# A spectral mixer on one core: the filter on four k1 low at once with 32x32 tiles, and the last two transforms in the other order

## The chip, the core and the metric

The kernel runs on one NeuronCore of a Trainium2 chip. The metric is the time of one execution on the device in microseconds, the median of several runs. The core's engines run side by side, each with its own queue of instructions: PE (TensorE, matmuls), DVE (VectorE), ACT (ScalarE), POOL (GpSimd) and SP (which here only issues transfers). PE reads from SBUF and writes to PSUM, which has eight banks of 128 partitions x 512 float32.

## The reference

The input x has 2048 tokens of 512 channels. Both branches start from its layer norm, and their product is added to x:

```
xn = layernorm(x)
s  = irfft2(rfft2(xn) * (w_r + 1j * w_i))          # over tokens and channels
h  = layernorm(xn)
u  = gelu(einsum("sd,sf->df", h, w1) + b1)          # mixing over the tokens, F = 1792
g  = silu((u @ w2 + b2).T)
out = x + s * g
```

## The kernel before

Tokens are split as 128 partitions times 16 tiles j (2048 = 128 x 16), so that the transform over the sequence falls into two steps: one of 128 points over the partitions, with the frequency k1 = 16 hi + lo (hi 0 to 3, lo 0 to 15, real and imaginary rows), and one of 16 points over j. The channel transform is done on 128 folded rows in four groups. The products with w1 and w2 are made from operands split in a high and a low part (float32r), three products for each; those of the spectral branch are plain float32, apart from the last transform.

First stage (16 passes, one for each j). Layer norm, the first seven of the 14 tiles of u (`hidden_early`, L335), the 128-point transform of h (`first_transform`, L207), and `fold`, whose two writes on DVE (L228) and two on POOL (L223, L224) leave the rows in `ey`.

Middle stage. PE works at two things in turn. `hidden_rest` gives the other seven tiles of u, as 32 parts of w1 (`w1_part`) with three or four groups of three products each (`mm3`, L118 to L120), prepared three parts ahead: a copy on ACT for the high half and a subtraction on DVE for the low one (`split`, L115). `filter_steps` is the filter of one of the 16 k1 low, in four steps: the channel transform (four matmuls of 128 columns, L446) and its copy by ACT (L448); the 16-point transform over j, one 128x128 matmul of 512 columns (L454), whose matrix `gf` serves all four hi at once; two half-height copies by ACT that swap real and imaginary rows (L456, L457); twelve operations on DVE that weight the rows (L465 to L482), with two more copies by ACT (L483, L484); and the transform back over j (four matmuls of 128 columns, L505), which ACT copies to `ey` (L506). A list of steps with weights says after which filter step how many groups of `hidden_rest` come, in the order of the code; the scheduler then orders the instructions of each engine.

Last stage (eight passes p over output tiles p and p + 8). Seven products of 21 matmuls with forms of w2 (L768); `w2_form` makes them from loads of w2 on SP (L609) and adding loads on POOL (L611). Between them stand, for each of 16 tiles j, `gathered` (a copy of the rows of tile j by ACT, L693), `channels` (the inverse channel transform, four matmuls, L700, and nine operations on DVE with a split, L115), `spectral` (the inverse 128-point transform as three float32r products, L118 to L120 again), and `finish`, which multiplies with the gate from PSUM (L739) and adds the tile to the output by a transfer on POOL (L741).

Of the kernel before, what the change touches and what calls it, by code (L numbers as in the profile page):

```python
# [8 lines left out]
F32 = mybir.dt.float32  # L9
# [15 lines left out]
TAIL = 2  # L25
# [4 lines left out]
RT = float(np.sqrt(0.5))  # L30

def _round12(a):
    m, e = np.frexp(a)
    return np.ldexp(np.round(m * 4096.0) / 4096.0, e)


def _parts(a, axis):
    hi = _round12(a)  # L40
    return np.stack([hi, a - hi], axis).astype(np.float32)


def _constants():
    q = np.arange(P)
    f = np.zeros((P, P))
    for lo in range(16):
        for hi in range(4):
            k = 16 * hi + lo
            a = 2 * np.pi * ((q * k) % P) / P  # L50
            f[:, lo * 8 + hi] = np.cos(a)
            f[:, lo * 8 + 4 + hi] = np.cos(np.pi * q) if k == 0 else np.sin(a)
# [19 lines left out]
    g = np.zeros((16, P, P))  # L72
    freq = np.zeros((P, 16), int)
    j = np.arange(16)
    for lo in range(16):
        for hi in range(4):
            k1 = 16 * hi + lo
            for r in range(16):
                re, im = r * 4 + hi, 64 + r * 4 + hi
                cr, sr = j * 8 + hi, j * 8 + 4 + hi  # L80
                if k1:
                    k = k1 + 128 * r
                    th = 2 * np.pi * ((j * k) % S) / S
                    g[lo, cr, re], g[lo, sr, re] = np.cos(th), -np.sin(th)
                    g[lo, cr, im], g[lo, sr, im] = -np.sin(th), -np.cos(th)
                    freq[[re, im], lo] = k
                elif r == 0:
                    g[lo, cr, re], g[lo, cr, im] = 1.0, np.cos(np.pi * j)
                    freq[im, lo] = S // 2
                else:  # L90
                    k = 128 * r if r < 8 else 64 + 128 * (r - 8)
                    rows = cr if r < 8 else sr
                    th = 2 * np.pi * ((j * k) % S) / S
                    g[lo, rows, re], g[lo, rows, im] = np.cos(th), -np.sin(th)
                    freq[[re, im], lo] = k
    c = {
        "c_f": f.astype(np.float32),
        "c_ft": _parts(f.T, 1),
        "c_d": fd.reshape(4, P, P).transpose(1, 0, 2).astype(np.float32),
        "c_i": iv.transpose(1, 0, 2).astype(np.float32),  # L100
        "c_g": g.astype(np.float32),
        "c_h": g.transpose(0, 2, 1).astype(np.float32),
# [4 lines left out]
def spectral_mixer_kernel(tc, x, w1, b1, w2, b2, wk, we, wx, c_f, c_ft, c_d, c_i, c_g, c_h, out):  # L107
# [14 lines left out]
    with tc.tile_pool(name="ps", bufs=1, space=PSUM) as psp, ExitStack() as left, ExitStack() as right:  # L122
# [463 lines left out]
        for step, lag in steps:  # L586
# [4 lines left out]
            if slot % 2:  # L591
                form_step()
# [250 lines left out]
```

## Time and profile before

| what | value |
|---|---|
| time, median of 3 runs | 394.23 us (394.01 to 394.5) |
| profiled execution, its span | 390.9 us |
| first stage | 0 to about 96 us |
| middle stage, filter and most hidden products | about 96 to 208 us |
| end of the hidden products, first forms | about 208 to 219 us |
| last stage, eight passes | about 219 us to the end, 20.7 us a pass |

The profiled execution's own time is its span; the median of the runs lies 3.3 us above it. A line such as L454 is line 454 of the kernel before. In a group's row stand the engine, the operation, the tiles written and read, the shape and the count, then busy time and the mean duration of one in ns, then the idle time of the engine ahead of it and what ended it. A stretch's row gives busy time and count for PE, PE's weight loads, DVE, ACT and POOL, then the granted clock, the share of the DMA engines and GB/s. A row of the chain gives start, length and what ran.

### The profile page before, as it was taken

What the parts mean: (1) busy time and instruction counts of PE and PEld (TensorE: products, weight loads), DVE (VectorE), ACT (ScalarE), POOL (GpSimd) and SP (SyncE); (2) the same over time, 40 slices, a digit from 0 to 9 for tenths busy, and PEclk for the clock granted to TensorE, in tenths of its full rate; (3) what the DMA queues carried; (4) which work ended last, traced back from release to release, by engine and by line L of the source; (5) the groups of instructions that cost most, each with busy time, mean ns of one, the idle gap of its engine ahead of it and who ended that gap; (6) DMA issues with size and microseconds to landing.
All of it is one profiled execution on the core that took longest, in us unless ns stands there. A gap on an engine that the chain in (4) does not pass through costs nothing.

```text
span 390.9 us, 7102 instructions
## 1 busy us (share of the span) xinstructions
PE 383.5 (98%) x2456; PEld 338.9 (87%) x2456; DVE 327.9 (84%) x776; ACT 248.3 (64%) x455; POOL 59.0 (15%) x109
## 2 busy tenths in 40 slices
PE   8999999999999999999999999999999999999995
PEld 4888888888787887788878889999999999999994
DVE  6899998866699989978898879797879788787974
ACT  4677665575987665687667486565646474656542
POOL 2133332322100000000011003020202011110200
PEclk9999999999999999999999999999999999999999
DMA  8957457213545535653637459887868778685602
GB/s 267 311 171 249 146 199 247 71 34 101 181 139 170 181 111 172 177 180 114 190 109 230 94 192 230 175 215 155 229 131 234 147 217 162 197 152 168 110 9 54
DMA packets 35016, 64.72 MB, mean 166 GB/s; under 512 B 4194, under 2 KB 19426, under 8 KB 34852
## 3 DMA queue, kind: packets, MB, share of 16 engines
q1 hardware_dynamic: 30292, 52.40, 42.1%
q0 software_dynamic: 4688, 11.86, 18.0%
q8 instruction: 19, 0.31, 0.3%
q14 instruction: 17, 0.14, 0.1%
HBM read 60.05 MB, written 8.13 MB: 174 GB/s over the span
## 4 chain that ended last, share of the span: by engine, by line
PE 88%; ACT 4%; DVE 4%; DMA 1%; issue 1%; SPq 0%; POOL 0%; DVEq 0%; ACTq 0%; POOLq 0%
PE ps L768 32%; PE ps L335 20%; PE ps L119 6%; PE ps L118 6%; PE ps L120 6%; PE ps L207 4%; PE ps L700 3%; PE ps L446 3%; PE ps L454 3%; PE ps L505 3%; PE ps L324 1%; ACT w2f L620 1%; DMA a<-in_w_dram 1%; DVE w2f L621 1%; ACT u L267 1%
## 5 line engine op out<-in xcount | busy, mean ns | idle before, releaser
L335 PE MATMUL ps<-h,w1h 128*128 128x512 f32 x224 | 58.5, 398 | 0.0
L118 PE MATMUL ps<-h,w1h 128*128 128x512 f32 x112 | 50.4, 451 | 0.1
L621 DVE TENSOR_TENSOR w2f<-s,w2f 128x896 fp32r<-128x896 f32 x32 | 34.8, 1092 | 17.5 <-ACT w2f L620 16.8
L335 PEld LDWEIGHTS ps<-h,w1h 128*128 128x128 f32 x224 | 40.9, 188 | 7.9
L120 PE MATMUL ps<-h,w1l 128*128 128x512 f32 x112 | 45.3, 405 | 0.0
L119 PE MATMUL ps<-h,w1h 128*128 128x512 f32 x112 | 44.3, 396 | 0.0
L768 PE MATMUL ps<-fa,w2f 128*128 128x256 f32 x336 | 43.4, 282 | 0.1
L768 PE MATMUL ps<-fb,w2f 128*128 128x256 f32 x336 | 42.7, 281 | 0.1
L768 PEld LDWEIGHTS ps<-fa,w2f 128*128 128x128 f32 x336 | 41.4, 188 | 0.9 <-DVE w2f L621 0.3
L768 PEld LDWEIGHTS ps<-fb,w2f 128*128 128x128 f32 x336 | 40.5, 188 | 0.5 <-DVE c L735 0.5
L768 PE MATMUL ps<-fc,w2f 128*128 128x256 f32 x336 | 40.7, 279 | 0.0
L768 PEld LDWEIGHTS ps<-fc,w2f 128*128 128x128 f32 x336 | 40.0, 188 | 0.0
L620 ACT ACTIVATE w2f<-s 128x896 fp32r<-128x896 f32 x32 | 30.2, 947 | 14.0 <-DVE s L634 10.3
L621 DVE TENSOR_TENSOR w2f<-a,w2f 128x896 fp32r<-128x896 f32 x24 | 26.0, 1085 | 6.1 <-ACT w2f L620 6.0
L620 ACT ACTIVATE w2f<-a 128x896 fp32r<-128x896 f32 x24 | 22.8, 950 | 12.7 <-PE ps L768 8.7
L335 PE MATMUL ps<-h,w1l 128*128 128x512 f32 x112 | 30.6, 390 | 0.0
L611 POOL DMA_DIRECT2D s<-in_w_dram x16 | 13.9, 869 | 106.8 <-DVE es L705 45.7
L118 PEld LDWEIGHTS ps<-h,w1h 128*128 128x128 f32 x112 | 21.2, 189 | 6.2 <-issue 2.6
L119 PEld LDWEIGHTS ps<-h,w1h 128*128 128x128 f32 x112 | 21.2, 189 | 5.5 <-issue 2.6
L120 PEld LDWEIGHTS ps<-h,w1l 128*128 128x128 f32 x112 | 21.0, 188 | 5.4 <-issue 1.0
L335 PEld LDWEIGHTS ps<-h,w1l 128*128 128x128 f32 x112 | 21.0, 188 | 4.5
L330 DVE TENSOR_TENSOR w1l<-w1r,w1h 128x512 fp32r<-128x512 f32 (+1 forms) x32 | 20.6, 644 | 2.7 <-ACT w1h L327 2.6
(126 smaller groups left out, 784.2 us busy)
## 6 DMA issues: line engine op xcount, KB each, us to landing
a<-in_w_dram SPq DMA_DIRECT2D x24, 448.0 KB, 3.5
wt<-in_wk_dram SPq DMA_DIRECT2D x16, 512.0 KB, 3.7
s<-in_w_dram POOLq DMA_DIRECT2D x17, 448.0 KB, 6.4
s<-in_w_dram SPq DMA_DIRECT2D x15, 448.0 KB, 3.9
w1s<-in_w_dram SPq DMA_DIRECT2D x48, 128.0 KB, 2.5
w1r<-in_w_dram SPq DMA_DIRECT2D x16, 256.0 KB, 3.4
x<-in_x_dram SPq DMA_DIRECT2D x15, 256.0 KB, 3.6
out_dram<-in_x_dram SPq DMA_DIRECT2D x4, 960.0 KB, 6.7
```

The source lines that it names most:

```text
L118: T.matmul(o, lh, rh, start=first, stop=False)
L119: T.matmul(o, lh, rl, start=False, stop=False)
L120: T.matmul(o, ll, rh, start=False, stop=last)
L207: T.matmul(z[:, b], h[:, b * P:(b + 1) * P], c, start=True, stop=True)
L330: keep(V.tensor_sub(dst, src, hi.bitcast(F32)))
L335: T.matmul(ps[:, bank + i], w[wi][:, i * P:(i + 1) * P], hj, start=first and j == 0, stop=last and j == NJ - 1)
L446: T.matmul(pd[:, b * P:(b + 1) * P], eyl[:, b], cd[:, b], start=True, stop=True)
L454: T.matmul(px, gf, sh, start=True, stop=True)
L611: G.dma_start(t, w2_half(*added), accum_op=ALU.add)
L620: ordered(A.activation(wf[:, 0], v, AF.Copy))
L621: ordered(V.tensor_sub(wf[:, 1], v, wf[:, 0].bitcast(F32)))
L768: in_turn(j0, T.matmul(o, wf[:, wi, i], ui, start=m + a == 0 and n in (1, 2, 5), stop=m == NH - 1 and a == 2, skip_group_check=n in (6, 3, ...
```

## The change

The filter now takes the 16 k1 low in four groups of four (`QUADS`, `filter_quad`). The rows of `ey` are laid out so that the 16 j (real, imaginary) of one hi stand on 32 partitions. The transform over j is then, for each of four lo and four hi, a matmul of 32x32 with 512 columns; the one back is 32 such matmuls with 256 columns. Where real and imaginary rows had been swapped by half-height copies, ACT copies two PSUM banks at once (`e`) and two transfers on SP exchange even and odd rows into `z`. DVE weights half a group at a time. Of the 32 parts of w1, 16 keep the subtraction on DVE; the others get their low half as a negated copy by ACT, to which a transfer on POOL adds w1. In the last stage the rows of a tile are collected by eight transfers (`gathered`), the 128-point transform comes first and in plain float32 (`sequence`), the channel transform follows, and `finish` reads SBUF.

```diff
+QUADS = ((4, 5, 6, 7), (0, 1, 2, 3), (8, 9, 10, 11), (12, 13, 14, 15))
...
-        ey = pers.tile([P, 16, 4, 16, 8], F32, name="ey")
+        ey = pers.tile([P, 16, 4, 8, NJ], F32, name="ey")
+        eys = ey.rearrange("p l g h j -> p l (g h j)")
...
-                keep(V.scalar_tensor_tensor(ey[:, :, g, j, :], t[:, 0].rearrange("p (l c) -> p l c", c=8), sc,
-                                            o[:, 0].rearrange("p (l c) -> p l c", c=8), op0=ALU.mult, op1=ALU.add))
+                keep(V.scalar_tensor_tensor(ey[:, :, g, :, j], t[:, 0].rearrange("p (l h) -> p l h", h=8), sc,
+                                            o[:, 0].rearrange("p (l h) -> p l h", h=8),
+                                            op0=ALU.mult, op1=ALU.add))
...
-        def filter_steps(n, lo):
...
+        def filter_quad(n, los):
+            gf = mp.tile([P, 4, 32], F32, name=f"gf{n}", tag="gf")
+            SY.dma_start(gf, c_g[n].rearrange("p (q c) -> p q c", c=32))
+            for q, lo in enumerate(los):
+                pd = ps[:, 6 - q]
+                for b in range(4):
+                    T.matmul(pd[:, b * P:(b + 1) * P], ey[:, lo, b].rearrange("p h j -> p (h j)"), cd[:, b],
+                             start=True, stop=True)
+                A.activation(eys[:, lo].rearrange("p (s g c) -> p g s c", s=2, c=64),
+                             pd.rearrange("p (g s c) -> p g s c", s=2, c=64), AF.Copy)
+                yield
+            for q, lo in enumerate(los):
+                for hi in range(4):
+                    T.matmul(ps[32 * q:32 * q + 32, 3 + hi], gf[32 * hi:32 * hi + 32, q], eys[32 * hi:32 * hi + 32, lo],
+                             start=True, stop=True)
...
+            def swapped(h):
+                e, z = (mp.tile([P, 2, 2, 256], F32, name=f"{c}{n}_{h}", tag="ez", bufs=4) for c in "ez")
+                A.activation(e, ps[:, 3 + 2 * h:5 + 2 * h].rearrange("p b (s c) -> p b s c", s=2), AF.Copy)
+                SY.dma_start(z[0::2], e[1::2])
+                SY.dma_start(z[1::2], e[0::2])
+                return e, z
+            def weighted(h, e, z):
...
+                for i, w in enumerate((wa, wb)):
+                    SY.dma_start(w, wk[:, at:at + 2, i::2])
...
+                G.tensor_mul(s1[:, 0], z[:, :, :, 0], e1[:, at:at + 2])
+                G.tensor_mul(s1[:, 1], e[:, :, :, 0], e2[:, at:at + 2])
+                G.tensor_add(s1[:, 0], s1[:, 0], s1[:, 1])
+                V.scalar_tensor_tensor(pr, zi, sg[:, 0:1], er, op0=ALU.mult, op1=ALU.add)
+                V.scalar_tensor_tensor(pi, zr, sg[:, 0:1], ei, op0=ALU.mult, op1=ALU.subtract)
+                V.tensor_mul(pq, pq, wa)
+                V.tensor_add(pr, pr, pi)
+                V.scalar_tensor_tensor(er, zi, sg[:, 1:2], er, op0=ALU.mult, op1=ALU.add)
+                V.scalar_tensor_tensor(ei, zr, sg[:, 1:2], ei, op0=ALU.mult, op1=ALU.subtract)
+                V.tensor_mul(e, e, wb)
+                V.tensor_add(er, er, ei)
+                V.tensor_sub(pi, pr, er)
+                V.tensor_add(pr, pr, er)
+                V.tensor_copy(pq[:, :, :, 0], s1[:, 0])
...
+            weighted(0, *swapped(0))
             yield
+            half = swapped(1)
             yield
+            weighted(1, *half)
             yield
+            for s in range(2):
+                for hi in range(4):
+                    for q in range(4):
+                        rows = slice(32 * q, 32 * q + 32)
+                        T.matmul(ps[32 * hi:32 * hi + 32, 3 + q, 256 * s:256 * s + 256], hf[rows, hi, s],
+                                 back[hi // 2][rows, hi % 2, s], start=True, stop=True)
...
-                    w.append(w1_part(*parts_[i + 3][:2], True))
+                    w.append(w1_part(*parts_[i + 3][:2], i % 3 == 0 or i + 3 >= len(parts_) - LATE // 3))
...
+        slots = [(0, 2)] * 4 + [(0, 2), (0, 2)]
+        for n in range(1, 4):
+            slots += [(n, 3), (n - 1, 2)] + [(n, 4)] * 3 + [(n, 3), (n, 3), (n - 1, 1)]
+        slots += [(3, 16), (3, 0)]
...
         def gathered(j):
+            yj = fp.tile([P, D], F32, name=f"yj{j}", tag="yj", bufs=3)
+            for r in range(8):
+                SY.dma_start(yj[16 * r:16 * r + 16], eys[16 * r + j:16 * r + j + 1])
+            return yj
+
+        def sequence(j, yj):
+            pf = ps[:, j // NP].rearrange("p (b c) -> p b c", c=P)
+            for b in range(4):
+                in_turn(j, T.matmul(pf[:, b], yj[:, b * P:(b + 1) * P], cft, start=True, stop=True))
             yt = fp.tile([P, 4, P], F32, name=f"yt{j}", tag="yt", bufs=2)
-            A.activation(yt.rearrange("p b (l c) -> p b l c", c=8), ey[:, :, :, j, :].rearrange("p l b c -> p b l c"), AF.Copy)
+            A.activation(yt, pf, AF.Copy)
             return yt
...
-            split(ch, cl, y)
-            return ch, cl
-
-        def spectral(j, y):
-            mm3(ps[:, j // NP], cft[:, 0], cft[:, 1], *y, True, True)
+            return y
...
-            V.tensor_mul(g[:, cols], ps[:, j // NP, cols], g[:, cols])
+            V.tensor_mul(g[:, cols], y[:, cols], g[:, cols])
```

How the order moves on PE in the second half of the middle stage: the rows before, where `h` and `w1h`, `w1l` belong to the hidden products, `sh` and `gf` to the transform over j, `pq` and `hf` to the one back.

```order
L454 MATMUL ps<-sh_2327,gf_2250 128x512
L120 MATMUL ps<-h_94,w1l_7_2333 128x512
L118 MATMUL ps<-h_94,w1h_7_2332 128x512
L119 MATMUL ps<-h_94,w1h_7_2332 128x512
L120 MATMUL ps<-h_94,w1l_7_2333 128x512
L118 MATMUL ps<-h_95,w1h_8_2379 128x512
L119 MATMUL ps<-h_95,w1h_8_2379 128x512
L120 MATMUL ps<-h_95,w1l_8_2380 128x512
L505 MATMUL ps<-hf_2269,pq_2282 128x128 x4
L118 MATMUL ps<-h_95,w1h_8_2379 128x512
```

The same engine with the change (line numbers are those of the changed kernel: L121 to L123 are the hidden products, L461 the 32x32 matmuls forward, L517 those back), first where the third group of four goes forward, then where the second comes back.

```order
L123 MATMUL ps<-h_100,w1l_13_1807 128x512
L461 MATMUL ps<-ey,gf_1732 32x512 x16
L121 MATMUL ps<-h_100,w1h_13_1806 128x512
L122 MATMUL ps<-h_100,w1h_13_1806 128x512
L123 MATMUL ps<-h_100,w1l_13_1807 128x512
```

```order
L123 MATMUL ps<-h_101,w1l_14_1832 128x512
L517 MATMUL ps<-pq_0_1646,hf_1628 32x256 x8
L517 MATMUL ps<-pq_1_1760,hf_1628 32x256 x8
L517 MATMUL ps<-pq_0_1646,hf_1628 32x256 x8
L517 MATMUL ps<-pq_1_1760,hf_1628 32x256 x8
L121 MATMUL ps<-h_101,w1h_14_1831 128x512
```

Where single matmuls of one k1 low stood every few products, there are now 16 or 32 small ones in a row, four times each way.

PE with the change at the end of the middle stage, where the back transform of the last four stands (`pq_0` and `pq_1` are its halves) and the last hidden products follow:

```order
L121 MATMUL ps<-h_99,w1h_12_2345 128x512
L517 MATMUL ps<-pq_1_2273,hf_2152 32x256 x8
L517 MATMUL ps<-pq_0_2163,hf_2152 32x256 x8
L517 MATMUL ps<-pq_1_2273,hf_2152 32x256 x8
L123 MATMUL ps<-h_101,w1l_14_2450 128x512
L121 MATMUL ps<-h_102,w1h_15_2456 128x512
L122 MATMUL ps<-h_102,w1h_15_2456 128x512
```

Before, the last back transform has this place; 45 products follow it to the first product of the last stage, and 19 with the change:

```order
L505 MATMUL ps<-hf_2397,pq_2410 128x128 x4
L118 MATMUL ps<-h_98,w1h_11_2467 128x512
L119 MATMUL ps<-h_98,w1h_11_2467 128x512
L120 MATMUL ps<-h_98,w1l_11_2468 128x512
L118 MATMUL ps<-h_98,w1h_11_2467 128x512
```

The queue of SP in a pass of the last stage, before (`s` and `a` are loads of w2) and with the change (`yj` are the collected rows):

```order
L609 DMA a_2_2970<-in_w_dram 128x896
L609 DMA a_2_3002<-in_w_dram 128x896
L609 DMA s_11_3223<-in_w_dram 128x896
L609 DMA s_2_3030<-in_w_dram 128x896
L609 DMA a_10_3080<-in_w_dram 128x896
```

```order
L621 DMA a_2_2891<-in_w_dram 128x896
L621 DMA a_2_2921<-in_w_dram 128x896
L706 DMA yj_2923<-ey 16x1x512 x8
L621 DMA s_2_2958<-in_w_dram 128x896
L621 DMA a_10_3004<-in_w_dram 128x896
L706 DMA yj_3035<-ey 16x1x512 x8
L621 DMA s_11_3156<-in_w_dram 128x896
```

Sixteen transfers of 32 KB join five loads, and stand behind loads that wait for a free buffer.

More of the change, by code (lines that the diff above doesn't have):

```diff
@@ L24 @@
 WARM = 16
-TAIL = 2
 LATE = 12
@@ L82, in _constants @@
                     k = k1 + 128 * r
+                    if k1 == 0 and r > 7:
+                        k = 64 + 128 * (r - 8)
                     th = 2 * np.pi * ((j * k) % S) / S
[L84 to L95, printed above, removed]
+                    if k1:
+                        g[0, :, re], g[1, :, re] = np.cos(th), -np.sin(th)
+                        g[0, :, im], g[1, :, im] = -np.sin(th), -np.cos(th)
+                        at[[re, im]] = k
+                    elif r == 0:
+                        g[0, :, re], g[0, :, im] = 1.0, np.cos(np.pi * j)
+                        at[im] = S // 2
+                    else:
+                        one = 0 if r < 8 else 1
+                        g[one, :, re], g[one, :, im] = np.cos(th), -np.sin(th)
+                        at[[re, im]] = k
@@ L96, in _constants @@
+                gf[n, 32 * hi:32 * hi + 32, q] = g.reshape(32, 32)
+                h = g.reshape(32, 32).T.copy()
+                t = np.empty_like(h)
+                t[0::2], t[1::2] = -h[1::2], h[0::2]
+                if k1 == 0:
+                    t[:2] = h[:2] = 0.5 * h[:2]
+                hf[n, 32 * q:32 * q + 32, hi] = np.stack([h, t], 1)
+    back = [lo * 8 + hi * 2 + s for hi in range(4) for s in range(2) for lo in range(16)]
+    sign = np.where(np.arange(P) % 2, 1.0, -1.0)
     c = {
@@ L572, in hidden_rest @@
                 gelu(ft, bank)
-        order = list(range(1, 6)) + [0] + list(range(6, 16))
-        chain = [filter_steps(n, lo) for n, lo in enumerate(order)]
+        chain = [filter_quad(n, los) for n, los in enumerate(QUADS)]
         rest = hidden_rest()
-        total, done, paced, slot = 16 * 7 - LATE, 0, 0, 0
-        steps = [(step, lag) for step in range(16 + 3) for lag in (0, 1, 3) if 0 <= step - lag < 16]
-        weight = {s_: TAIL if s_[0] > 15 else 1 for s_ in steps}
-        whole_weight = sum(weight.values())
-        next(chain[0])
+        slots = [(0, 2)] * 4 + [(0, 2), (0, 2)]
+        for n in range(1, 4):
+            slots += [(n, 3), (n - 1, 2)] + [(n, 4)] * 3 + [(n, 3), (n, 3), (n - 1, 1)]
+        slots += [(3, 16), (3, 0)]
+        total = 16 * 7 - LATE
         for ft, bank in ((9, 6), (2, 2), (8, 5), (1, 1), (7, 4), (0, 0)):
@@ L585, in spectral_mixer_kernel @@
         waiting = [[(3, 3)]]
-        for step, lag in steps:
-            if lag == 0 and step + 1 < 16:
-                next(chain[step + 1])
-            next(chain[step - lag])
-            slot += 1
-            if slot % 2:
-                form_step()
-            paced += weight[step, lag]
-            while done * whole_weight < paced * total:
+        done, given, whole_weight = 0, 0, sum(k for _, k in slots)
+        for n, k in slots:
+            form_step()
+            next(chain[n], None)
+            given += k
+            while done * whole_weight < given * total:
                 next(rest)
```

178 lines of the change are left out of this document (71 added, 107 removed).

## The prediction

> **What bounds the kernel now.** I read the page's busy times first, then the busy times of the engines in stretches cut at the stages, then the chain that ended last in order of time, and last the groups by line and the DMA issues.
>
> ```profile
> span 390.9 us, 7102 instructions
> PE 383.5 (98%) x2456; PEld 338.9 (87%) x2456; DVE 327.9 (84%) x776; ACT 248.3 (64%) x455; POOL 59.0 (15%) x109
> core 0: us, PE busy (x) PEld busy (x) DVE busy (x) ACT busy (x) POOL busy (x), PEclk, DMA share, GB/s
> 96.00:206.70 110.70, 110.20 (x576) 88.82 (x575) 99.83 (x254) 81.80 (x153) 7.13 (x24) 1.00 0.52 157
> 206.70:235.00 28.30, 26.93 (x176) 24.11 (x175) 23.32 (x39) 20.19 (x34) 1.46 (x2) 1.00 0.59 176
> 266.85:287.37 20.52, 20.52 (x171) 20.12 (x171) 16.72 (x33) 12.06 (x20) 3.46 (x4) 1.00 0.78 183
> ```
>
> In the middle stage, where the filter runs (96 to 206.7 us), PE is busy for 110.2 of 110.7 us, at the full granted clock (1.00); in one pass of the last stage for all of 20.52. DVE stands at 99.8 of 110.7 and would be the next bound. PE idles for 7.4 us in the whole span, so to first order the time is the sum of what PE does. What a matmul costs there is the distance from one start to the next, which the chain gives:
>
> ```profile
> 98.19 0.23 PE ps L118
> 107.71 0.86 PE ps L454 x2
> 109.72 0.89 PE ps L446 x8
> 121.04 0.89 PE ps L505 x8
> 254.46 4.95 PE ps L768 x42
> 266.00 0.39 PE L118 MATMUL ps<-ch,cft 128*128 128x512 f32 x1
> 266.68 1.58 PE L768 MATMUL ps<-fa,w2f 128*128 128x256 f32 x12
> ```
>
> One float32 matmul is two records: 0.86 us for 512 columns, so 0.43 a record, and 0.89 us for four matmuls of 128 columns, so 0.11 a record. A product in float32r is one record, 0.23 us at 512 columns. The three products of the last sequence transform take 0.68 us (266.00 to 266.68). A product of the last stage is 21 records of L768, half of 4.95 us.
>
> **The change, part by part.** The sum is made against the profiled execution: span 390.9 us, with 3.3 us around it to the median of 394.2.
>
> *Removed from PE.* In the middle, for each of 16 k1 low, one forward sequence transform (L454) and four back (L505): 16 x 0.86 = 13.8 and 16 x 0.89 = 14.2, together 28.0 us. In the last stage, 16 x 0.68 = 10.9 us.
>
> *Added to PE, last stage.* Sixteen sequence transforms in plain float32, four matmuls of 128 columns each, by the row of L446 0.89 us: 14.2. Net +3.3 us, 0.41 in each of eight passes, and nothing covers it since PE is dense there.
>
> *Added to PE, middle.* Four times, 16 matmuls of 32x32 tiles with 512 columns forward, and 32 with 256 columns back. The trace has no matmul on less than the whole array, so this is bounded from both sides. If all 16 tiles run side by side, a forward group takes one matmul, 0.86 us, and a back group two rounds of 0.43, 0.86 as well: 8 x 0.86 = 6.9 us. If nothing overlaps, each group is 13.8 us, 110 in all. What else a group needs is weights:
>
> ```profile
> L454 PE MATMUL ps<-sh,gf 128*128 128x512 f32 x32 | 16.5, 598 | 0.4 <-ACT w1h L115 0.3
> L505 PEld LDWEIGHTS ps<-hf,pq 128*128 128x128 f32 x128 | 17.1, 191 | 2.5 <-issue 1.2
> L505 PE MATMUL ps<-hf,pq 128*128 128x128 f32 x128 | 17.2, 275 | 0.0
> ```
>
> A load of 128 columns keeps up with one record every 0.11 us, so one of 32 columns should need about a quarter, 0.028 us: 32 loads of a forward group 0.9 us, 64 of a back group 1.8. I take 1.0 and 1.8 us, 4 x 2.8 = 11.2. A record lasts 275 ns where the next starts after 111, so if the array had to run empty whenever it changes between whole and split, each change would cost 0.16 us. The order has the small matmuls in 13 groups, 26 changes, 4.3 us at most, and I take 2. Why the case near the lower end: each matmul of a round has a tile of its own, no two share both rows and columns of the array, and the code changes the rows and the PSUM bank at each matmul.
>
> The Trainium skill, "TensorE: Matmul & The Clock Gate", section "Measured speedup vs the span model", gives 10.6 times for 16 tiles with 512 columns. An estimate by that page makes a forward group 13.8 / 10.6 = 1.3 us, and the sum by it would be some 1 us longer. No run here shows it yet.
>
> So PE in the middle: -28.0 + 11.2 + 2.0 = -14.8 us.
>
> *DVE and ACT, middle.* These must stay under PE's new 96 us or so.
>
> ```profile
> L465 DVE TENSOR_TENSOR xc<-ps,zi 128x256 f32<-128x256 f32 x16 | 6.7, 418 | 4.7 <-ACT zi L457 4.7
> L470 DVE TENSOR_TENSOR xc<-xc,wt 128x1024 f32<-128x1024 f32 x16 | 19.6, 1225 | 0.0
> L471 DVE TENSOR_TENSOR xc<-xc 128x512 f32<-128x512 f32 x16 | 10.9, 684 | 0.0
> L480 DVE TENSOR_TENSOR s<-ps,e 128x2 f32<-128x2 f32 x16 | 2.4, 151 | 0.0
> L115 DVE TENSOR_TENSOR w1l<-w1s,w1h 128x512 fp32r<-128x512 f32 x16 | 11.0, 695 | 1.7 <-ACT w1h L115 1.6
> L115 DVE TENSOR_TENSOR w1l<-w1s,w1h 128x384 fp32r<-128x384 f32 x16 | 8.8, 552 | 0.6 <-ACT w1h L115 0.6
> L702 ACT ACTIVATE od<-ps 128x256 f32<-128x256 f32 x16 | 6.1, 380 | 1.1 <-PE ps L700 0.7
> L448 ACT ACTIVATE sh<-ps 128x512 f32<-128x512 f32 x16 | 9.5, 596 | 5.4 <-PE ps L446 5.3
> ```
>
> Before, each k1 low takes DVE six operations of 256 elements (2.5), one of 1024 (1.23), one of 512 (0.68) and three small ones (0.45): 4.9 us, 16 times 78. After, each half of a four takes eight of 512 (5.5), two of 1024 (2.45) and a small copy (0.15): 8.1 us, eight times 65. Sixteen of the 32 splits of w1 leave DVE, 8 x 0.70 + 8 x 0.55 = 10 us. DVE goes from 99.8 to about 77, 19 under PE. ACT loses four half-height copies (2.0 us) of each k1 low and gains eight copies of 1024 elements (from 380 and 596 ns by the slope 1.03 each, 8.2 us) and 16 negated copies of w1 (about 9): it falls from 82 to about 67. Both are covered by PE; without that cover they would be worth nothing here.
>
> *The strided writes of ey in the first stage.*
>
> ```profile
> 0.00:96.00 96.00, 94.64 (x472) 77.78 (x473) 79.85 (x239) 59.62 (x124) 25.93 (x55) 1.00 0.54 179
> L228 DVE SCALAR_TENSOR_TENSOR ey<-t,o 128x128 f32<-128x128 f32 x32 | 7.8, 283 | 0.8 <-ACT o L225 0.8
> ```
>
> DVE's two writes for each x tile (L228), and POOL's two, now step 64 bytes between elements. If they took twice as long, DVE would be busy for 88 of 96 us and POOL for 43: covered, 0. If they took less, also 0.
>
> *New transfers.*
>
> ```profile
> x<-in_x_dram SPq DMA_DIRECT2D x15, 256.0 KB, 3.6
> gf<-in_c_g_dram SPq DMA_DIRECT2D x16, 64.0 KB, 1.8
> out_dram<-g POOLq DMA_DIRECT2D x15, 256.0 KB, 4.3
> s<-in_w_dram POOLq DMA_DIRECT2D x17, 448.0 KB, 6.4
> L611 POOL DMA_DIRECT2D s<-in_w_dram x16 | 13.9, 869 | 106.8 <-DVE es L705 45.7
> L609 SPq DMA_DIRECT2D s<-in_w_dram x15: 327/328/554, 208.6 to 357.3; - x15
> ```
>
> The exchange of even and odd rows is two transfers of 256 KB for each half; by the rows of x and gf it lands in 1.8 to 3.6 us, and I take 3.6. The w1 loads and the weights wk queue behind it on SP, because it waits there for ACT's copy e. For quads 1 and 2 PE has about 27 us of work between the forward group and the back group, against 1.0 + 0.3 + 3.6 + 16.1 of copy, issue, landing and DVE: covered. For the last four PE has 86 products (19.6 us) and the back group of the third (1.8), 21.4 us, before the back transform that needs the second half; the chain there has five splits and forms more on DVE, 1.0 + 0.3 + 3.6 + 16.1 + 2.5 = 23.5. That is 2 us of waiting, with 1 more for the first four, whose copies compete with the gelu on ACT: +3, bounds 0 and 12.
>
> The collected rows of the last stage are 16 transfers of 32 KB in a pass. At 0.33 us an issue, eight take 2.6 us, and they land about 2 us later, 4.6 in all, while each is asked for at least two products (4.95 us) ahead. They wait for free buffers behind the w2 loads, so SP has them in hand; I take 0. The DMA share of that stage, 0.78, leaves room for 0.5 MB more on 3.8 (183 GB/s x 20.5 us), about 0.88. What they cost if that room is gone is in the third rival.
>
> **Sum:** -14.8 + 3.3 + 3 = -8.5 us, so a span of 382.4 and a time of 385.7 us. With all tiles together, no changes paid and no wait it is -28.0 + 6.9 + 3.3 = -17.8, 376.4; with 4.3 for the changes and 12 of waiting +2.8, 397.
>
> **The rivals.** *Pairs in order (slower).* Each float32 matmul is two records on the same tile, and the second cannot enter its tile before the first has streamed. If PE starts matmuls strictly in program order, the next tile's first record starts only beside this tile's second one. Then a forward group takes 17 x 0.43 = 7.3 us and a back group 33 x 0.215 = 7.1, four times 14.4 = 57.6 for 28.0: +29.6 + 3.3 = +32.9, 427 us. It decides from the point where a group takes more than 24.7 / 8 = 3.1 us. For it speaks that records start in order throughout the trace; against it, that a record of 275 ns has its next one started after 111, so PE takes work before the last is out. The Trainium skill says it too ("TensorE: Matmul & The Clock Gate", section "The mechanism"): matmuls keep program order in start and end, and only weight loads are pulled ahead.
>
> *Four at a time (slower).* Only tiles in different rows overlap: 16 / 4 x 0.86 = 3.44 us forward, 32 / 4 x 0.43 = 3.44 back, 27.5 us for 28.0. With changes 2, last stage 3.3 and 1 of waiting: +5.8, 400 us.
>
> *New waits eat it.* Half of the w1 parts now get their low half by two ACT copies, a POOL issue of 0.87 us and an adding transfer; landing 4.3 to 6.4 us by the two POOL rows, 6.4 to 8.5 in all. A part is prepared three ahead, 3 x 2.1 to 2.7 us of products plus PE's filter work, 8 to 10. POOL also stands at the small sums that wait for the exchanged rows, and the next adding transfer stands behind them. If each of 16 parts is half a microsecond late, 8 us are gone: 394. The same is reached by 1 us a pass of late rows in the last stage.
>
> **How the numbers follow.** Forecast 0.60, pairs in order 0.14, four at a time 0.12, new waits 0.14. The range from 376.4 to 403 holds the forecast's own bounds, the waits and nearly all of four at a time, and leaves out the pairs (0.14) and some 0.04 more. A measurement tells about 0.2% (0.8 us). Faster: 0.58 of the forecast and 0.06 of the waits, 0.64. Within 0.2%: 0.04. Slower: the two tile rivals 0.26 and 0.06 of the others, 0.32.
>
> **What would show it.** The 16 forward matmuls in about 1 us, not 3.4 or 7.3; the middle stage 12 us shorter; a pass of the last stage 20.9 instead of 20.5; DVE with idle time in the middle. PE waiting for the pq of the last four by more than 4 us, for w1l, or for yj would make the prediction wrong on the waits.

## The result and the profile after

| | median | range | ratio to before (95%) |
|---|---|---|---|
| before | 394.12 us | 393.06 to 394.5, 4 runs | |
| changed | 433.4 us | 431.72 to 435.79, 4 runs | 1.101 (1.097 to 1.105) |

The change makes the kernel 10% slower; 385.7 us were forecast, with a range up to 403. One run each of e13_s4first and e16_slots (433.55 and 430.65 us) fell in a slower state of the chip, and the medians below leave it out. The profiled execution took 431.72 us, with a span of 429.7. The page of the changed kernel (span, busy times, and the rows of PE, of the granted clock and of DMA in 40 slices):

```profile
span 429.7 us, 7703 instructions
PE 388.2 (90%) x2760; PEld 336.7 (78%) x2760; DVE 304.5 (71%) x646; ACT 220.4 (51%) x397; POOL 99.7 (23%) x138
...
PE   8999999999999948978697359999998999989995
...
PEclk9999999999999969989789598999999999999999
DMA  8856383126578666777654358899799999989812
```

PE, dense before, has holes from the 15th slice (150 us) on, and its granted clock falls in the same place. It is busy for 4.7 us more than before (383.5) and idle for 41.5 us instead of 7.4: 4.7 + 34.1 is the 38.8 us by which the span grew. Where they lie is seen from the stretches, cut where the last back transform ends and where the first product with `fb`, a good way into the last stage, begins; the changed kernel first, then the one before:

```profile
96.00:227.00 131.00, 113.97 (x840) 83.39 (x839) 90.31 (x149) 64.56 (x115) 45.98 (x51) 0.93 0.68 190
227.00:265.30 38.30, 24.57 (x149) 22.76 (x150) 19.82 (x29) 18.71 (x31) 2.95 (x4) 0.82 0.55 108
265.30:429.70 164.40, 155.00 (x1304) 152.53 (x1302) 113.98 (x231) 77.33 (x129) 24.66 (x29) 1.00 0.82 177
```

```profile
96.00:209.00 113.00, 112.50 (x590) 90.88 (x589) 101.83 (x257) 83.16 (x156) 7.13 (x24) 1.00 0.53 158
209.00:235.60 26.60, 25.23 (x168) 22.65 (x166) 21.92 (x37) 19.43 (x32) 1.72 (x2) 1.00 0.56 179
235.60:390.90 155.30, 151.08 (x1233) 147.55 (x1232) 124.34 (x247) 86.07 (x145) 24.17 (x28) 1.00 0.71 161
```

The middle stage is 18 us longer, the change of stages 12, the last stage 9; up to 96 us nothing moved. The small matmuls are not the cause. The timeline of PE in the changed kernel, for the second four's forward and the first four's back transform:

```profile
129.57 1.14 PE L461 MATMUL ps<-ey,gf 32*32 32x512 f32 x32
130.64 0.50 PE L121 MATMUL ps<-h,w1h 128*128 128x512 f32 x1
...
134.94 2.14 PE L517 MATMUL ps<-pq,hf 32*32 32x256 f32 x64
137.01 0.50 PE L121 MATMUL ps<-h,w1h 128*128 128x512 f32 x1
```

From start to start they take 1.07 and 2.07 us, where one tile after another would be 13.8: on average some 13 tiles run side by side forward, and some 7 back. What the engines wait for instead (engine, line, what it waited for: us in all, times, longest), from the list of waits between 96 and 230 us:

```profile
POOL s L621 <- PE ps L517: 19.6, 1, 19.6
DVE pq L493 <- PE ps L122: 11.7, 1, 11.7
ACT w1h L118 <- DMA w1s<-in_w_dram: 9.3, 5, 6.7
PE ps L123 <- DVE w1l L118: 8.8, 2, 6.5
PE ps L123 <- DMA w1l<-w1s: 6.7, 3, 3.6
```

In the middle PE waits for low halves of w1, of both kinds, 15.5 us in all. From PE's list over the whole span come two more, at the change of stages and in the last stage:

```profile
PE ps L785 <- ACT fd L277: 8.8, 1, 8.8
PE ps L712 <- DMA yj<-ey: 7.4, 4, 4.4
```

These four rows are 31.7 us of PE's 41.5 us of idle time. How the longest of the waits in the middle comes about is seen in the timelines of ACT, DVE, POOL and PE, in this order:

```profile
139.47 0.63 ACT L118 ACTIVATE w1h<-w1s 128x512 fp32r<-128x512 f32 x1 [0.33 <-DMA w1s<-in_w_dram]
```

```profile
143.39 0.41 DVE L486 SCALAR_TENSOR_TENSOR wb<-wb 2x256 f32<-2x256 f32 x1 [5.41 <-POOL wb L485]
143.73 0.73 DVE L493 SCALAR_TENSOR_TENSOR pq<-z,sg,e 128x512 f32<-128x512 f32 x1
...
154.86 0.73 DVE L498 SCALAR_TENSOR_TENSOR e<-z,sg,e 128x512 f32<-128x512 f32 x1
155.53 0.67 DVE L118 TENSOR_TENSOR w1l<-w1s,w1h 128x512 fp32r<-128x512 f32 x1
```

```profile
143.90 13.49 POOL L490 TENSOR_TENSOR s<-z,e 128x4 f32<-128x4 f32 x1 [0.54 <-DMA z<-e]
157.47 0.65 POOL L492 TENSOR_TENSOR s<-s 128x4 f32<-128x4 f32 x1
158.06 1.77 POOL L542 DMA_DIRECT2D w1l<-w1s  x2
```

```profile
156.25 0.80 PE L123 MATMUL ps<-h,w1l 128*128 128x512 f32 x1 [6.48 <-DVE w1l L118]
...
162.91 0.50 PE L123 MATMUL ps<-h,w1l 128*128 128x512 f32 x1 [1.79 <-DMA w1l<-w1s]
```

The high half is ready at 140.1, and its split needs 0.67 us of DVE. But DVE first waits 5.4 us (the exchange, and POOL's correction of two rows, stand ahead), and then runs the weights of one half and six operations of the next, 143.7 to 155.5, ahead of it in its order. Over the same time POOL, whose like sum took 0.19 us at 142.18, needs 13.49 us for a sum of 4 elements; the next two adding transfers stand behind it, and PE waits for them at 162.9.

### The profile page after: what moved, and what is told of

Same layout as the page of the kernel before. It is cut to its first block, busy times and chain, and to the rows that moved or that the text cites. A ratio compares the mean times of both kernels' runs of the same rounds, so it can differ in the third digit from the quotient of the medians.

```text
span 429.7 us, 7703 instructions
## 1 busy us (share of the span) xinstructions
PE 388.2 (90%) x2760; PEld 336.7 (78%) x2760; DVE 304.5 (71%) x646; ACT 220.4 (51%) x397; POOL 99.7 (23%) x138
## 4 chain that ended last, share of the span: by engine, by line
PE 53%; DMA 17%; DVE 14%; SPq 6%; issue 5%; ACT 4%; POOL 1%; DVEq 0%; ACTq 0%; POOLq 0%
PE ps L785 21%; PE ps L340 18%; DMA yj<-ey 4%; SPq L706 4%; DMA w1l<-w1s 4%; PE ps L211 3%; PE ps L712 3%; DMA w1s<-in_w_dram 3%; DVE w2f L633 2%; DMA wa<-in_wk_dram 2%; PE ps L721 2%; DMA z<-e 2%; DVE pq L495 2%; PE ps L329 1%; ACT w2f L632 1%
## 5 line engine op out<-in xcount | busy, mean ns | idle before, releaser
L123 PE MATMUL ps<-h,w1l 128*128 128x512 f32 x112 | 45.7, 422 | 15.7 <-DVE w1l L118 8.8
L340 PE MATMUL ps<-h,w1h 128*128 128x512 f32 x224 | 58.5, 398 | 0.0
L121 PE MATMUL ps<-h,w1h 128*128 128x512 f32 x112 | 47.2, 423 | 0.4 <-ACT u L272 0.4
L340 PEld LDWEIGHTS ps<-h,w1h 128*128 128x128 f32 x224 | 40.9, 188 | 7.9
L785 PE MATMUL ps<-fa,w2f 128*128 128x256 f32 x336 | 46.4, 294 | 0.0
L122 PE MATMUL ps<-h,w1h 128*128 128x512 f32 x112 | 45.6, 408 | 0.0
L785 PEld LDWEIGHTS ps<-fa,w2f 128*128 128x128 f32 x336 | 43.8, 201 | 0.0
L785 PE MATMUL ps<-fc,w2f 128*128 128x256 f32 x336 | 41.7, 280 | 0.0
L123 PEld LDWEIGHTS ps<-h,w1l 128*128 128x128 f32 x112 | 22.1, 199 | 23.8 <-DVE w1l L118 9.2
L785 PE MATMUL ps<-fd,w2f 128*128 128x256 f32 x168 | 23.8, 289 | 9.8 <-ACT fd L277 8.8
L121 PEld LDWEIGHTS ps<-h,w1h 128*128 128x128 f32 x112 | 22.3, 199 | 10.2 <-issue 5.0
L785 PEld LDWEIGHTS ps<-fd,w2f 128*128 128x128 f32 x168 | 21.2, 190 | 10.9 <-ACT fd L277 9.0
L756 POOL DMA_DIRECT2D out_dram<-g x15 | 13.5, 897 | 62.2 <-DVE g L754 53.8
```

What stands on the lines that cost most here:

```text
L121: T.matmul(o, lh, rh, start=first, stop=False)
L122: T.matmul(o, lh, rl, start=False, stop=False)
L123: T.matmul(o, ll, rh, start=False, stop=last)
L340: T.matmul(ps[:, bank + i], w[wi][:, i * P:(i + 1) * P], hj, start=first and j == 0, stop=last and j == NJ - 1)
L756: G.dma_start(out[:, j, cols], g[:, cols], accum_op=ALU.add)
L785: in_turn(j0, T.matmul(o, wf[:, wi, i], ui, start=m + a == 0 and n in (1, 2, 5), stop=m == NH - 1 and a == 2, skip_group_check=n in (6, 3, ...
```

## Experiments

Each is the changed kernel with the edit shown, or a combination. Columns: median, ratio to before with 95% interval; then from the profile of that run the start of the last back transform, of the first and last product with `fb`, and the span. The kernel before lay between 393.2 and 394.1 us.

| run | median | ratio | last back | first fb | last fb | span |
|---|---|---|---|---|---|---|
| before | 394.1 | | 208.7 | 235.6 | 386.5 | 390.9 |
| changed | 433.4 | 1.101 (1.097, 1.105) | 226.6 | 265.3 | 425.3 | 429.7 |
| e1_direct | 419.5 | 1.065 (1.062, 1.069) | 211.7 | 251.6 | 411.7 | 416.1 |
| e8_wkonce | 424.1 | 1.077 (1.074, 1.081) | 216.6 | 256.4 | 416.8 | 421.6 |
| e4_noz | 430.5 | 1.093 (1.088, 1.097) | 225.3 | 264.1 | 424.9 | 429.4 |
| e3_nogather | 420.5 | 1.068 (1.065, 1.071) | 227.3 | 259.2 | 413.1 | 417.5 |
| e13_s4first | 428.7 | 1.091 (1.084, 1.098) | 229.0 | 264.2 | 426.6 | 431.0 |
| e5_one | 423.2 | 1.076 (1.073, 1.078) | 228.8 | 262.5 | 417.1 | 421.5 |
| e9_wkpool | 439.9 | 1.118 (1.115, 1.121) | 230.9 | 270.3 | 433.4 | 438.1 |
| e20_direct_once | 415.2 | 1.057 (1.053, 1.061) | 207.2 | 247.3 | 407.3 | 412.4 |
| e16_slots | 426.8 | 1.084 (1.079, 1.088) | 219.5 | 261.2 | 421.6 | 426.1 |
| e26_sums_dve | 425.6 | 1.081 (1.078, 1.084) | 220.5 | 258.9 | 420.9 | 425.5 |
| e14_combo | 407.3 | 1.035 (1.033, 1.037) | 212.1 | 247.5 | 401.6 | 405.9 |
| e17_combo_slots | 403.3 | 1.026 (1.023, 1.029) | 209.4 | 242.5 | 399.0 | 403.4 |
| e18_ya | 399.9 | 1.015 (1.010, 1.019) | 207.9 | 236.8 | 393.9 | 398.3 |
| e24_best | 401.8 | 1.021 (1.020, 1.023) | 212.7 | 240.4 | 396.9 | 401.2 |
| e25_pooladd | 404.0 | 1.028 (1.025, 1.032) | 215.1 | 242.7 | 397.7 | 402.1 |
| e27_combo_sums | 400.8 | 1.016 (1.014, 1.019) | 209.3 | 236.2 | 395.2 | 399.6 |
| e21_noweights | 386.6 | 0.982 (0.980, 0.984) | 196.5 | 223.7 | 380.2 | 384.5 |
| e22_pe_only | 383.7 | 0.975 (0.974, 0.977) | 196.1 | 224.0 | 377.9 | 382.4 |

### One cause at a time

**No adding transfers.**

```diff
-                    w.append(w1_part(*parts_[i + 3][:2], i % 3 == 0 or i + 3 >= len(parts_) - LATE // 3))
+                    w.append(w1_part(*parts_[i + 3][:2], True))
```

> The changed kernel, but every part of w1 is split by ACT and DVE as in the kernel before, none by two ACT copies and an adding transfer. Theory Q (the middle waits because the weights wk have two buffers and stand on SP's queue ahead of the w1 loads, and the exchange with them): the chain through wa, DVE and SP stays, the last back transform ends at 220 us or later (227.0 in the changed kernel, 208.8 before), total 424 to 433 us. Theory P (the adding transfers bring the low halves late): PE's waits for w1l go, the last back transform ends at 205 to 212 us and the total is 410 to 418 us.

13.9 us less, and the last back transform at 211.7, at the top of theory P's range. PE's waits for low halves between 96 and 230 us fall from 15.5 to 2.7 us. The total is 1.5 us above that theory's figure: what follows the last back transform takes 204.4 us instead of 203.1.

**Weights wk loaded once** (seven of eight loads left out).

```diff
+        once = []
...
-                wa, wb = (mp.tile([P, 2, 2, 256], F32, name=f"w{c}{n}_{h}", tag="wt", bufs=2) for c in "ab")
-                for i, w in enumerate((wa, wb)):
-                    SY.dma_start(w, wk[:, at:at + 2, i::2])
+                if not once:
+                    once.extend(mp.tile([P, 2, 2, 256], F32, name=f"w{c}", tag="wt", bufs=2) for c in "ab")
+                    for i, w in enumerate(once):
+                        SY.dma_start(w, wk[:, at:at + 2, i::2])
+                wa, wb = once
```

> The changed kernel, but the weights wk of the first half are loaded once and used for all eight halves; seven of eight loads of wa and wb are left out. Theory Q: DVE no longer waits for wa, SP no longer stands at a load that waits for a buffer, and the last back transform ends at 210 to 217 us, total 415 to 423 us. Theory P: at most 3 us less than the changed kernel, 429 to 434 us.

9.3 us less, 1 short of theory Q's range but far from P's 3: theory Q has a part too. How large is open: in the changed kernel DVE waits only 2.6 us for wa, and in this run POOL's long sum is gone as well (the longest takes 1.06 us), which by itself is worth 7.8 us (e26_sums_dve, below). So neither theory is the whole. Both edits together:

> The changed kernel, all parts of w1 split by ACT and DVE, and the weights wk loaded once for all halves (seven of eight loads of wa and wb left out). If the adding transfers (13.9 us) and the wait for the two buffers of wk (9.3 us) are two delays one behind the other, 408 to 413 us; if they cover the same waits, 415 us or more.

415.2 us, 18 below the changed kernel where the two singly gave 23. The two overlap by 5 us, as the second case has it. Loading wk from another queue does not help:

```diff
-                    SY.dma_start(w, wk[:, at:at + 2, i::2])
+                    G.dma_start(w, wk[:, at:at + 2, i::2])
```

> The changed kernel, but the loads of the weights wk are issued by GpSimd instead of SP. Theory Q (they hold up the w1 loads and the exchange behind them on SP): SP no longer stands at them, the last back transform ends at 215 to 222 us instead of 227.0, total 420 to 427 us. If GpSimd's queue, with the adding transfers behind them, only takes over the stall: 430 us or more.

6.5 us more: POOL's queue, with the adding transfers on it, is worse than SP's. More buffers for wk were not tried.

**No exchange of rows.**

```diff
-                SY.dma_start(z[0::2], e[1::2])
-                SY.dma_start(z[1::2], e[0::2])
+                A.activation(z, ps[:, 3 + 2 * h:5 + 2 * h].rearrange("p b (s c) -> p b s c", s=2), AF.Copy)
```

> The changed kernel, but the exchange of even and odd rows is left out: z is a second copy of the same rows by ACT (eight more copies of 1 us). If the exchange's landing (four pieces of 3.9 to 4.2 us on the chain in the middle) is what the weights chain waits for, the last back transform ends at 213 to 219 us, total 418 to 426 us. If the exchange is hidden behind the wait for wa and for the w1 parts, 429 us or more.

2.9 us less, and the intervals touch. But a copy of 1 us a half took the exchange's place, and PE waits 7.4 us in all for these copies, so this does not price the exchange.

**No collected rows**, and one transfer a tile instead of eight.

```diff
-            for r in range(8):
-                SY.dma_start(yj[16 * r:16 * r + 16], eys[16 * r + j:16 * r + j + 1])
-            return yj
+            return eys[:, j]                    # e3_nogather
...
+            SY.dma_start(yj, eys[j::16])        # e5_one
```

> The changed kernel, but the sixteen tiles of collected rows are not collected: the last sequence transforms read rows of ey as they stand, without the 128 transfers. If the transfers are late (theory G), the first sequence transform starts 5 to 8 us earlier, PE's waits for yj go, the last stage (first to last product with fb) takes 153 to 155 us instead of 159.9, total 418 to 426 us. If the last stage is longer by its products or by the w2 loads, it stays at 158 us or more and the total is above 428 us.

> The changed kernel, but each tile of collected rows is collected by one transfer (eight rows to 128) instead of eight (one row to 16). Theory I (eight issues of 0.63 us stand on SP's queue, with the w2 loads between them): most of the 12.9 us that leaving the collection out gave comes back, total 419 to 424 us. Theory L (the landing, with each row read from one partition, is what is late, or the 0.5 MB of each pass): the waits for yj stay, 428 us or more.

Leaving them out gives 12.9 us: from first to last `fb` 153.9 us instead of 160.0, and the first `fb` 31.9 us behind the last back transform instead of 38.7. One transfer in place of eight brings back 10.2 of these. SP's timeline of the changed kernel, and of e14_combo with one transfer a tile, says how:

```profile
250.32 10.07 SPq L706 DMA_DIRECT2D yj<-ey  x16
260.50 0.53 SPq L621 DMA_DIRECT2D s<-in_w_dram  x1
```

```profile
235.06 1.39 SPq L706 DMA_DIRECT2D yj<-ey  x2
236.50 0.90 SPq L621 DMA_DIRECT2D s<-in_w_dram  x1
```

Two tiles hold SP's queue for 10.1 us, 0.63 for each issue, and the loads of w2 stand behind them; with one transfer a tile it is 1.4 us. PE's waits for the collected rows fall from 7.4 to 2.2 us in e5_one. Theory I holds.

**Place of s4 in memory.**

```diff
+        w2p.tile([P, NH * P], F32, name="s4_place", tag="s4", bufs=1)
         nxt = {"s1": s1_load(0, w2p, G), ...
```

> The changed kernel, but in the pool of the second weights the tile of s4 is placed first, so that s1's load (on GpSimd's queue) reuses memory whose last reader is DVE, and s4's load takes the place whose last reader is the last back transform. Theory T (placement: s1 waits for the last back transform, 19.6 us on POOL, its form comes late, and the copies queued behind it on ACT make PE wait 8.8 us for fd): that wait goes, from the first product with fd to the first with fb 24 to 28 us instead of 34.0, total 421 to 426 us. If the wait comes from the copies and splits themselves in their order, no change: 429 us or more.

s1's load no longer waits for the last back transform (19.6 us before, now 11.8 for DVE), 4.3 of PE's 8.8 us for `fd` go, and the first `fb` comes 35.2 us behind the last back transform instead of 38.7. From the first `fd` to the first `fb` it is 30.4 us where 24 to 28 were expected. The total misses its range too: the runs spread from 426.9 to 432.7 us, the profiled one is the slowest of these with a middle stage 2.4 us longer, and the interval of the ratio overlaps that of the changed kernel. The wait is shown, its price is not.

**Spacing of the fours**, and **GpSimd's sums on DVE**.

```diff
-            slots += [(n, 3), (n - 1, 2)] + [(n, 4)] * 3 + [(n, 3), (n, 3), (n - 1, 1)]
-        slots += [(3, 16), (3, 0)]
+            slots += [(n, 3), (n - 1, 2), (n, 4), (n, 3), (n, 3), (n, 3), (n, 2), (n - 1, 1)]
+        slots += [(3, 25), (3, 0)]              # e16_slots
...
-                G.tensor_mul(s1[:, 0], z[:, :, :, 0], e1[:, at:at + 2])
+                V.tensor_mul(s1[:, 0], z[:, :, :, 0], e1[:, at:at + 2])    # e26_sums_dve, and five more
```

> The changed kernel, but the three later quads follow one another after 21 products instead of 24, so that 25 products instead of 16 lie under the last quad's weights. Theory S (the order of the work leaves too few products under the last chain): the last back transform ends at 216 to 222 us instead of 227.0, total 421 to 428 us. If the chain of transfers, DVE and the parts of w1 sets the pace by itself, the waits only move, 430 us or more.

> The changed kernel, but GpSimd's small sums of the middle stage (three of 4 elements a half, and three operations on two rows) are given to DVE, 0.15 us each there. Theory G (GpSimd is held up while DVE runs its weights one behind another: one sum of 4 elements lasts 13.49 us in the changed kernel, from 143.90 to 157.39, and the adding transfers of w1 stand behind it): the adding transfers issue when ACT is done, PE's 6 to 8 us of waiting around 150 to 163 us shrink, total 418 to 427 us. If the sums only wait for what they read, and the 13.49 us is a matter of how the trace shows GpSimd, 430 us or more.

6.6 and 7.8 us less. The second one is a cause that no theory had until the traces showed the 13.49 us: with the sums off POOL, the two adding transfers issue at 149.64 instead of 158.06, PE's longest wait for such a transfer falls from 3.6 to 1.6 us, and PE's busy time from 388.2 to 384.6. The wait of 6.5 us for the split on DVE stays (6.95 in this run).

### Together

> The changed kernel with three edits together: all w1 parts split by ACT and DVE, each tile of collected rows by one transfer, s4 placed first. If the three delays lie one behind another (middle, change of stages, last stage), their gains add up: 13.9 + 8 to 12 + 5 to 8, total 398 to 406 us, still behind the kernel before. If they cover one another, 408 us or more.

> The three edits together (parts of w1 split by ACT and DVE, one transfer for collected rows, s4 placed first; 407.3 us) and the same spacing of 21 and 25 products. Theory S: 399 to 404 us, the last back transform ends at 205 to 209 us. If DVE is full in that stretch (21 of 22 us busy from 190 to 212 in the run with three edits) the spacing does nothing: 406 us or more.

> The run before this one, and the first tile of collected rows has memory of its own (yj two buffers instead of three), and is asked for before the loads of the last stage on SP's queue instead of behind them. If the first sequence transform of the last stage waits for SP and the memory it frees (first transform at 240.8 us with three edits, where the products stand from about 235), 4 to 6 us less than the run before this one, 395 to 400 us. If the wait only moves to the next tile or to the forms of w2, less than 2 us.

```diff
+        ya = w2p.tile([P, D], F32, name="ya", tag="ya", bufs=1)
...
+        SY.dma_start(ya, eys[0::16])
         fp = pool(left, "left", "fin", 1)      # e18_ya
```

407.3, 403.3 and 399.9 us. The three edits gain 26.1 us together, where singly they gave 28.9 (13.9, 10.2, and 4.8 that is not clear of the noise): nearly all of it adds up, and 407.3 lies between the two cases. The spacing is worth 4.0, and the first tile's early request 3.4, a little less than expected. What still holds PE in the middle stage of the last one is told by two runs in which DVE's weights are left out, with one copy by ACT in their place. e21_noweights is e18_ya without them, as shown here; e22_pe_only is the changed kernel with all parts of w1 split by ACT and DVE, s4 first and the new spacing, and without weights, exchange, loads of wk and collected rows.

```diff
-                V.scalar_tensor_tensor(pr, zi, sg[:, 0:1], er, op0=ALU.mult, op1=ALU.add)
...
-                V.tensor_copy(pq[:, :, :, 0], s1[:, 0])
+                A.activation(pq, e, AF.Copy)
```

> The run with five edits (399.9 us), but the eleven DVE operations that weight each half are left out (one ACT copy of e to pq stands in for them); exchange, loads of wk and GpSimd's small sums stay. If DVE is now what the middle stage waits for (weights, splits and forms in one queue, 16 to 19 of 20 us busy), the last back transform ends at 196 to 202 us instead of 207.9 and the total is 389 to 395 us. If the transfers and ACT's copies set the pace, 205 us or later and 397 us or more.

> The changed kernel with all that PE could wait for taken away and its own instructions left as they are: the exchange, the loads and the use of wk and the collected rows are left out (one ACT copy of e stands in for the weights, the last sequence transforms read rows of ey as they stand), all w1 parts are split by ACT and DVE, s4 is placed first, 21 and 25 products between the quads. If the prediction's sum for PE is right (-14.8 in the middle, +3.3 in the last stage), the last back transform ends at 194 to 199 us (208.8 before), PE is busy for 370 to 374 us (383.5 before, 388.2 in the changed kernel), and the total is 381 to 388 us. If the 32x32 matmuls or the float32 transforms cost PE more than forecast, or the slower clock comes with them and not with the waits, 392 us or more.

Both come out as the first case of each says, e21_noweights even below its range: 386.6 and 383.7 us, less than the kernel before. The stretches of e21_noweights, and of e18_ya that has the weights:

```profile
96.00:197.00 101.00, 99.90 (x825) 76.21 (x824) 39.90 (x77) 63.84 (x108) 10.97 (x37) 1.00 0.68 216
```

```profile
96.00:208.30 112.30, 102.49 (x822) 76.71 (x820) 95.87 (x161) 54.83 (x97) 37.54 (x37) 0.98 0.58 187
```

With exchange and loads in place, 216 GB/s and all, PE is dense in 101 us as soon as DVE has not the weights. With them DVE is busy for 95.9 of 112.3 us, and PE idles for 9.8. The run takes away more than DVE's time, though: SP's loads of wk, which in e18_ya wait 18.7 us for DVE's products with wk (L495, L499), no longer do, and POOL's sums take 0.38 us at most instead of 15.11. Page and groups of e22_pe_only confirm the sum for PE:

```profile
PE 372.9 (98%) x2760; PEld 329.7 (86%) x2760; DVE 252.5 (66%) x572; ACT 217.9 (57%) x389; POOL 56.9 (15%) x95
```

```profile
L461 PE MATMUL ps<-ey,gf 32*32 32x512 f32 x128 | 6.6, 600 | 0.0
L491 PE MATMUL ps<-pq,hf 32*32 32x256 f32 x256 | 6.0, 385 | 0.0
```

372.9 us with the same 2760 instructions as in the changed kernel, where 383.5 - 14.8 + 3.3 = 372.0 was forecast.

**Three more tries to pass the kernel before**: 18 products between the fours and 34 under the last one, with a third buffer for the collected rows (e24_best); the spacing of e18_ya, the third buffer, and one addition of each half on GpSimd (e25_pooladd) or GpSimd's sums on DVE (e27_combo_sums).

```diff
-                V.tensor_add(pr, pr, pi)
+                G.tensor_add(pr, pr, pi)               # e25_pooladd
```

> The run with five edits, three buffers for the collected rows again (the last x tile takes the first one's own memory), and 18 products between the quads instead of 21, 34 under the last. If the wait for pq at the end of the middle (4.8 us) and the third buffer (last stage 157.1 us from fb to fb, 154.1 with three) are what is left, 394 to 398 us. If DVE is full, the wait for pq only moves to w1l, and the total stays at 398 us or more.

> The run with five edits (399.9 us; spacing of 21 and 25 products), three buffers for the collected rows again, and one of the ten additions of each half (pr + pi, 0.68 us on DVE) given to GpSimd. If DVE's queue is what the middle waits for, 5.4 us less on it are worth 2 to 5 us: 395 to 398 us. If GpSimd takes 1.5 us or more for it (its 4-element products take 2.3 us in the changed kernel) and the chain of one half, not DVE's load, sets the pace, 400 us or more.

> The run with five edits (399.9 us; spacing of 21 and 25 products), three buffers for the collected rows, and GpSimd's small sums of the middle stage given to DVE. Theory G: the first half's and the second half's back transforms no longer wait for the sums behind DVE's operations, 393 to 398 us, about the kernel before. If DVE's load or the chain of one half is what is left, 399 us or more, since DVE gets 3.6 us more to do.

401.8, 404.0 and 400.8 us: none helps. The third buffer was not run by itself. The addition takes 1.7 us on POOL where DVE took 0.68, so the chain of a half grew while DVE's load fell by 5.4 us, and the middle stage became 7 us longer. The fastest version that computes the reference, e18_ya, stays 1.5% behind the kernel before.

## Why the prediction was wrong

**PE's own work: right.** In e22_pe_only the small matmuls take 6.6 + 6.0 = 12.6 us against 11.2 + 2.0, and all of PE's work 372.9 us against 372.0. That the 12.6 comes so close is in part luck: a whole forward group takes 1.07 us as forecast, but the first four go forward in three pieces of about 1.05 us each, while a back group takes 1.42 there instead of 1.8. The last stage costs 3.0 us more from first to last `fb` without the collected rows (e3_nogather, 153.9 against 150.9; 0.41 for each of somewhat over seven passes was forecast). With nothing to wait for the kernel takes 9.7 us less than before. Both rivals on the tiles fall. By the Trainium skill ("TensorE: Matmul & The Clock Gate", section "Measured speedup vs the span model") the prediction estimated 1.3 us for a forward group; the trace has 1.07.

**"That is 2 us of waiting, with 1 more for the first four ... +3, bounds 0 and 12": this step failed.** PE idles for 34 us more. For each four the prediction laid one chain (copy, exchange, 16.1 us of DVE) beside PE's products and called it covered, as if DVE, POOL and SP served that chain alone and the products needed nothing from them. But the products that were to cover the chain need w1 parts, and these pass through the same three queues: the splits stand on DVE behind the weights (15.4 us from 140.1 to 155.5 for a split of 0.67), the adding transfers on POOL behind a sum of 13.49 us, the w1 loads on SP behind the loads of wk, which wait there 13.1 us for DVE's products with wk. Splits and adding transfers together are 15.5 us of PE's waiting. The cover waited for what it was to cover. DVE's load itself was well estimated: the weights were put at 65 us, and the groups of L493 to L503 add up to 66.2 (two of 9.7, four of 5.9, four of 5.4 to 5.5, one of 1.3). "Both are covered by PE" is true of such totals (DVE is busy for 90.3 of 131 us) and says nothing of the order.

**"I take 0" for the collected rows: wrong by 12.9 us.** An issue was priced by a load from another line, 0.33 us; these take 0.63, so that two tiles hold SP for 10.1 us, the loads of w2 wait behind them, and PE waits 7.4 us for the rows. And the first two tiles, though asked for early in the code, have buffers in memory that the last forms free: SP issues them from 250.3 us on, when PE wants them (memory of its own and an earlier request for the first tile gave 3.4 us in e18_ya).

**The change of stages, 11.8 us longer, stood in no term.** The load of s1 takes memory that the last back transform reads (POOL waits 19.6 us for L517), its form comes late, and PE waits 8.8 us for `fd` behind it. The first part of this is shown by e13_s4first, its price is not. The order had shown that 19 matmuls instead of 45 follow the last back transform; what those 45 had covered was not asked.

**"New waits eat it", 394 us, chance 0.14: the right rival at a sixth of its size.** It named the adding transfers and even POOL's small sums, and priced half a microsecond for each of 16 parts, 8 us. The adding transfers alone cost 13.9 us, and all that e22_pe_only takes away costs 49.7 (433.4 - 383.7).

**A long wait is paid twice.** PE's busy time is 15.3 us larger in the changed kernel than in e22_pe_only, for the same instructions. Its timeline shows how:

```profile
212.05 0.79 PE L123 MATMUL ps<-h,w1l 128*128 128x512 f32 x1 [3.63 <-DMA w1l<-w1s]
212.64 0.63 PE L122 MATMUL ps<-h,w1h 128*128 128x512 f32 x1
213.07 0.63 PE L123 MATMUL ps<-h,w1l 128*128 128x512 f32 x1
...
217.31 0.39 PE L121 MATMUL ps<-h,w1h 128*128 128x512 f32 x1
217.53 0.40 PE L122 MATMUL ps<-h,w1h 128*128 128x512 f32 x1
```

After a wait of 3.63 us products start 0.43 us apart instead of 0.23, for 5 us, and the stretches with waits have a clock of 0.82 to 0.93. After the wait of 6.48 us (156.25, above) it takes 3 us until they stand 0.23 us apart again, and after that of 1.79 us (162.91) hardly two products. The Trainium skill says so ("TensorE: Matmul & The Clock Gate", section "What's actually happening"): half rate after an idle window of about 3.4 us, full rate after as long a busy one. The trace agrees. The prediction priced waits at their length alone.

**Strided writes of `ey`: right at 0.** PE is busy for 94.66 us of the first 96, before 94.64.

**What stays open.** Why e18_ya's middle stage, though DVE has 16 us to spare there in all, ends hardly earlier than before (207.9 against 208.7): whether DVE's load at its end (forms, splits and weights of the last four in one queue) or the length of a half's chain sets the pace. e25_pooladd made the one smaller and the other longer, and lost; e24_best and e27_combo_sums moved the wait and gained nothing. Nor is it shown what makes POOL's one sum last 13.49 us: it lasts so only while DVE runs the weights, but not every time that it does (last section).

## What to carry to other kernels

Before calling a chain covered, list what the covering instructions need, and look for the same queues in both lists: a cover that is fed by the chain's own engines is none. Price a new operation on a shared queue by all that stands behind it, and a transfer by the issue of its own shape. A packing of small matmuls can be as good as promised (12.6 us for 28.0) and still lose, since the work that it moves to DVE, POOL and transfers (66 us of weights) has to end in a fixed order with everything else there.

## What the runs showed of the hardware

A sum of 4 elements on POOL lasted 13.49 us in the changed kernel, 16.07 in e1_direct and 15.11 in e18_ya, each time while DVE ran tensor operations one behind another; the same kind of sum takes 0.19 us at 142.18, with DVE idle. Without DVE's weights (e21_noweights) none lasts over 0.38 us. A busy DVE alone does not make the long sum: in e8_wkonce, with DVE busy for 14.9 of 15.0 us (143 to 158), the same sum took 0.70. From POOL's timeline, the short sum in the changed kernel, the long ones in e1_direct and e18_ya, and the ones of e8_wkonce and e21_noweights:

```profile
142.18 0.19 POOL L490 TENSOR_TENSOR s<-z,e 128x4 f32<-128x4 f32 x1
```

```profile
140.84 16.07 POOL L490 TENSOR_TENSOR s<-z,e 128x4 f32<-128x4 f32 x1 [2.19 <-DMA z<-e]
```

```profile
139.50 15.11 POOL L490 TENSOR_TENSOR s<-z,e 128x4 f32<-128x4 f32 x1 [1.28 <-DMA z<-e]
```

```profile
144.32 0.70 POOL L494 TENSOR_TENSOR s<-z,e 128x4 f32<-128x4 f32 x1
```

```profile
178.88 0.38 POOL L492 TENSOR_TENSOR s<-s 128x4 f32<-128x4 f32 x1
```

Spans on POOL are rough, but what follows on its queue starts after them, and taking the sums off POOL gave 7.8 us. A transfer from one partition to 16 takes SP 0.63 us to issue, one from eight partitions to 128 takes 0.70: here the number of issues counts for SP's queue, not the bytes.
